# Long convolution and two dense layers on one core: four of sixteen weight chunks are decoded during the transform of u

## The chip, the core and the metric

The kernel runs on one core of a Trainium2 chip, as one launch. The metric is device time in microseconds, 1407.19 us as the median of three runs before the change. TensorE (PE), VectorE (DVE), ScalarE (ACT) and GpSimd (POOL) compute, each in its own fixed order of instructions; SyncE (SP) issues all DMAs, also in a fixed order, so that a DMA that has to wait holds up those behind it.

## The reference

```python
h_filt = (np.maximum(pos_emb @ w1, 0.0) @ w2) * np.exp(-0.01 * np.arange(S))[:, None]
u = x * v                                            # S = 12480 rows, D = 128 columns
y = np.fft.irfft(np.fft.rfft(u, n=2*S, axis=1) * np.fft.rfft(h_filt, n=2*S, axis=0)[None], n=2*S, axis=1)[:, :S]
x = (x * y).reshape(S, D)
h = np.maximum(x @ moe_w_in, 0.0); x = (h * h) @ moe_w_out            # 128 -> 2048 -> 128
h = x @ moe2_w_in                                                     # again 128 -> 2048 -> 128
return np.where(h > 0.0, h, np.exp(np.minimum(h, 0.0)) - 1.0) @ moe2_w_out
```

The four weight matrices arrive in float64, the rest in float32.

## The kernel before

The work has three phases.

**Phase 1** (`phase1`) is the first stage of the transforms. x and v come in 16 parts j of 8 columns each (`load_xv(j)`), into rotating buffers `xc` (x, ten of them) and `vc` (v, two of them; the first eight parts of v lie in tiles `m` that are written only later). `ufold(j)` multiplies and folds a part in three DVE instructions (lines 265, 266, 267; the last one is recorded at line 130). `s1(i)` is a group of 16 matmul records on PE (line 274) whose results ACT copies out of PSUM. There are 16 groups for the filter, then 32 for u, two for each part j. Ten parts are folded ahead of the groups for u, and after the groups of part j, part j + 10 is loaded and folded into the buffers that have come free. `prologue` issues eight small loads (`w2`, `g` and six of `tb`) after group 15, and the first matmuls of phase 2 after groups 24 and 29.

**Phase 2** (`phase2`) is a loop over 46 pairs p of frequencies. For each pair PE computes `u` (line 452, two PSUM buffers) and, two pairs later, the inverse stage `v` (line 475). In even pairs it also computes `rt` (line 319), in odd ones `h` (line 332) from `rr`, the copy that ACT makes of `rt`. ACT also copies `h` to `hh` and `v` to `z`; SP stores `z`. `prod(p)` is two products on DVE (lines 464, 465) and two sums on POOL (lines 467, 468), which give `pt` for `v`. DVE must have read `u` of pair p before PE can write `u` of pair p + 2, and `rr` must be copied before the next `h`.

Between these instructions a generator `weights()` puts the work on the 16 weight chunks (512 KB of float64 each, read as pairs of 32-bit words, `low` and `high`). It is stepped four times in each pair, once before `prod`, once after it, and twice more, and each step emits the next piece of one `decode` and of one `split`. `decode(c)` makes float32 out of the words: DVE masks the mantissa (373), ACT scales it (375), DVE shifts the exponent out (376), ACT limits it in two steps (379, 382), DVE adds the low word (381) and the sign (384), POOL multiplies mantissa and power (389). `split(c)` makes the high and low halves for the matmuls: ACT copies (recorded at 133, `m<-wf`), POOL subtracts (130, `m<-wf,m`). Decode c starts at step 11c or later, with at most four decoded chunks waiting for their split (`wf`, four buffers); splits start in pairs 8, 16 and 32, when the tiles `m` come free. Raw chunks have two buffers, and chunk c + 2 is loaded when DVE has last read chunk c. The order of instructions on each engine is the order in which the program writes them (`manual_schedule`).

The tiles of phase 2 (`raw`, `pt`, `m2`, `z` and others, pool `p2b`) lie in the memory of pool `xv`, which holds `xc` and `vc` in phase 1.

**Phase 3** (`phase3`) is the end of the inverse transform and the two layers, eight steps for each of 26 tiles of rows; it is not touched.

Of the kernel before, what the change touches and what calls it, by code (L numbers as in the profile page):

```python
# [10 lines left out]
F32 = mybir.dt.float32  # L11
F32R = mybir.dt.float32r
U32 = mybir.dt.uint32
AF = mybir.ActivationFunctionType
ALU = mybir.AluOpType
# [5 lines left out]
D = 128  # L21
# [9 lines left out]
R = 99  # L31
# [1 line left out]
SIZES = (4,) + 24 * (5,) + (3,)  # L33
KTAIL = K1 - 64
TBB = 6
WF = 4
PD = NP - 2
PZ = PD - 4
HD = (33, 35, 36, 37, 38, PZ + 2)
# [1 line left out]
WDEC = 11  # L41
OFF = 3
LAG1 = 2
NX = 10
NV = 2
NWARM = 6
NS1 = 55

# [71 lines left out]
class Build:  # L120
# [56 lines left out]
    def phase1(self):  # L177
        nc, a = self.nc, self.a
        with ExitStack() as ctx1:
# [5 lines left out]
            ns = [0]  # L185
# [15 lines left out]
            xvp = self.right.enter_context(self.tc.tile_pool(name="xv", bufs=1, side="right"))  # L201
# [10 lines left out]
            def load_xv(j):  # L212
                for i, (d, nm, n) in enumerate(((xs, "xc", NX), (vs, "vc", NV))):
                    if i and j < 8:
                        t = self.xu[j // 4][:R, 1024 * (j % 4):1024 * (j % 4) + 1024]
                    else:
                        t = xvp.tile([R, 1024], F32, tag=nm, name=nm, bufs=n)
                    d[j] = t.rearrange("p (d h n) -> p d h n", d=8, h=2)
                    for b, e in ((0, R - 1), (R - 1, R)):
                        nc.sync.dma_start(out=t[b:e], in_=a["xv"][j, i, b:e])  # L220
# [10 lines left out]
            for j in range(8):  # L231
                load_xv(j)
# [30 lines left out]
            def ufold(j):  # L263
                x, v = xs[j], vs.pop(j)
                nc.vector.tensor_tensor(out=v, in0=x, in1=v, op=ALU.mult)
                nc.vector.tensor_tensor(out=x[:, :, 0], in0=v[:, :, 0], in1=v[:, :, 1], op=ALU.add)
                self.sub(nc.vector, x[:, :, 1], v[:, :, 0], v[:, :, 1])

            def s1(i, fb, dst, w):
                ps = stile(2, 512)  # L270
                pv = ps[:, :, :4 * K1].rearrange("p b (c e) -> p b c e", e=2)
                for j in range(4):
                    for q, (b, e) in enumerate(((0, C1), (C1, N2))):
                        nc.tensor.matmul(pv[b:e, j // 2, :, j % 2], lhsT=fb[j][q], rhs=self.t1[:, :, q:q + 2],  # L274
                                         start=(j % 2 == 0), stop=(j % 2 == 1))
                b = 0
                for o, n in dst:
                    o = o.rearrange("p (c d) -> p c d", d=w)[:N2, :, 4 * i:4 * i + 4]
                    o, z = o.rearrange("p c (b e) -> p c b e", e=2), pv[:N2, :, b:b + n].rearrange("p b c e -> p c b e")
                    self.copy(o, z)  # L280
                    b += n

            for j in range(NX):
                ufold(j)
                if 8 <= j + 8 < NX:
                    load_xv(j + 8)
            for i in range(E // 4):
                s1(i, [(fold[:, 0, :, 4 * i + c], fold[:, 1, 1:, 4 * i + c]) for c in range(4)], [(self.xr, 2 * K1)], E)
            dst = [(t, n) for t, n in zip(self.xu + [self.xt], (32, 32, 64, 2 * KTAIL))]
            self.raw = {}  # L290
            for j in range(D // 8):
                x = xs.pop(j)
                for i in range(2 * j, 2 * j + 2):
                    s1(i, [(x[:, 4 * (i % 2) + c, 0], x[:, 4 * (i % 2) + c, 1, 1:]) for c in range(4)], dst, D)
                    self.prologue(i)
                if j + NX < D // 8:
                    load_xv(j + NX)
                    ufold(j + NX)

    def buf(self, tag, shape, bufs, dt=F32, pool=None):  # L300
        return (pool or self.p2).tile([128] + list(shape), dt, tag=tag, name=tag, bufs=bufs)
# [50 lines left out]
        if i == 29:  # L352
            self.hmm(0)

    def load_weights(self, c):
        l, k, q = c // 8, c // 4 % 2, c % 4
        raw = self.buf("raw", [4, D, 2], 2, U32, self.p2b)
        src = self.a[(("moe_w_in", "moe_w_out"), ("moe2_w_in", "moe2_w_out"))[l][k]].bitcast(U32)
        if k == 0:
            src = src[:, 1024 * q:1024 * q + 1024].rearrange("p (b d) -> p b d", d=2 * D)  # L360
        else:
            src = src[512 * q:512 * q + 512, :].rearrange("(b p) d -> p b d", p=128)
        self.nc.sync.dma_start(out=raw.rearrange("p a b c -> p a (b c)"), in_=src)
        self.raw[c] = raw

    def decode(self, c):
        nc = self.nc
        raw = self.raw.pop(c)
        low, high = raw[:, :, :, 0], raw[:, :, :, 1]
        e = self.buf("we", [4, D], 2, U32, self.p2b)  # L370
        f = self.buf("wf", [4, D], WF, pool=self.p2b)
        t, s, w, m = e.bitcast(F32), e, f, f.bitcast(U32)
        nc.vector.tensor_scalar(out=m, in0=high, scalar1=0xFFFFF, scalar2=None, op0=ALU.bitwise_and)
        yield
        nc.scalar.activation(out=f, in_=m, func=AF.Copy, scale=2.0 ** -20, bias=1.0)
        nc.vector.tensor_scalar(out=e, in0=high, scalar1=1, scalar2=21,
                                op0=ALU.logical_shift_left, op1=ALU.logical_shift_right)
        yield
        nc.scalar.activation(out=t, in_=e, func=AF.Relu, bias=self.ebias[:, 0:1], scale=-1.0)
        yield  # L380
        nc.vector.scalar_tensor_tensor(out=f, in0=low, scalar=2.0 ** -52, in1=f, op0=ALU.mult, op1=ALU.add)
        nc.scalar.activation(out=e, in_=t, func=AF.Relu, bias=self.ebias[:, 1:2], scale=-8388608.0)
        yield
        nc.vector.scalar_tensor_tensor(out=s, in0=high, scalar=0x80000000, in1=e,
                                       op0=ALU.bitwise_and, op1=ALU.bitwise_or)
        if c + 2 < 16:
            self.load_weights(c + 2)
        yield
        nc.gpsimd.tensor_tensor(out=w, in0=f, in1=s.bitcast(F32), op=ALU.mult)  # L389
        yield  # L390
        self.dec[c] = w

    def split(self, c):
        if c % 4 == 0:
# [11 lines left out]
        yield  # L406

    def weights(self):
        self.w, self.dec = {}, {}
        nd = ns = 0  # L410
        gd = gs = None
        i = 0
        while ns < 16 or gs is not None:
            if gd is None and nd < 16 and nd - ns < WF and i >= WDEC * nd:
                gd, nd = self.decode(nd), nd + 1
            if gs is None and ns < 16 and ns in self.dec and self.pair >= (8, 16, 32, 32)[ns // 4]:
                gs, ns = self.split(ns), ns + 1
            if gd is not None and next(gd, 0) == 0:
                gd = None
            if gs is not None and next(gs, 0) == 0:  # L420
                gs = None
            i += 1
            yield

    def phase2(self):
        nc, a, st = self.nc, self.a, self.st
        ctx0 = self.ctx
        with ExitStack() as self.ctx:
# [6 lines left out]
            x0 = self.x0pool.enter_context(self.tc.tile_pool(name="x0", bufs=1, side="right"))  # L435
            self.x0 = [x0.tile([128, n0 * (R - 1)], F32R, name=nm) for nm in ("xh0", "xl0")]
            self.p2b = p2b = self.right.enter_context(self.tc.tile_pool(name="p2b", bufs=1, side="right"))
            for c in range(2):
                self.load_weights(c)
            wgen = self.weights()  # L440

# [53 lines left out]
            n = sum(nrs)  # L495
# [358 lines left out]
```

## Time and profile before

| | us |
|---|---|
| median of three runs (lowest, highest) | 1407.19 (1406.85, 1408.92) |
| the profiled execution | 1408.68 |
| its span in the trace | 1406.9 |
| PE busy (share of the span) | 1372.3 (98%) |
| DVE, ACT, POOL busy | 1187.2, 1128.8, 615.3 |

The profiled execution is 1.5 us above the median of the runs, and its span is 1.8 us shorter than its time. Phase 1 ends near 91 us and phase 2 near 237 us. Records of PE are pipelined, so that their durations overlap; starts tell more than ends. A number in square brackets behind a row is the time its engine was idle ahead of it, with what ended that.

### The profile page before, as it was taken

The numbers are of one execution on the slowest core, as the hardware profiler recorded it, in microseconds if no ns is written. First come the engines' busy times: TensorE is split into PE (matmuls) and PEld (weight loads), VectorE is DVE, ScalarE is ACT, GpSimd is POOL, SyncE is SP. The second block draws the span as 40 slices with busy tenths as digits, with TensorE's granted clock in tenths as the row PEclk, the third lists the DMA queues.
The fourth block names the chain that finished last, engine by engine and source line by source line (L and its number), as shares of the span: only waits on it lengthen the run. The fifth ranks groups of instructions, "written<-read, shape, count | busy, mean of one in ns | idle before, by whom it ended". The sixth has DMA issues, their size and how long they took to land.

```text
span 1406.9 us, 19203 instructions
## 1 busy us (share of the span) xinstructions
PE 1372.3 (98%) x7240; PEld 1157.6 (82%) x7240; DVE 1187.2 (84%) x1259; ACT 1128.8 (80%) x1484; POOL 615.3 (44%) x341
## 2 busy tenths in 40 slices
PE   8999898999999999999999999999999999999997
PEld 7986665898888888888888888888888888888875
DVE  6648786789888898888988898898988898888887
ACT  5777665788888888888888888888888888888886
POOL 3028784644444444444444444444444444444431
PEclk9999999999999999999999999999999999999999
DMA  8746674201110111001110111001110111000000
GB/s 264 191 121 205 167 249 138 87 0 41 41 41 1 42 41 41 16 26 41 41 42 0 41 42 41 19 24 41 41 41 1 41 41 42 16 13 9 8 8 12
DMA packets 43165, 81.49 MB, mean 58 GB/s; under 512 B 3944, under 2 KB 32755, under 8 KB 43073
## 3 DMA queue, kind: packets, MB, share of 16 engines
q1 hardware_dynamic: 43073, 80.27, 18.9%
q8 instruction: 57, 0.93, 0.3%
q14 instruction: 35, 0.29, 0.1%
HBM read 61.90 MB, written 18.32 MB: 57 GB/s over the span
## 4 chain that ended last, share of the span: by engine, by line
PE 89%; DVE 3%; POOL 2%; ACT 2%; DMA 2%; issue 1%; SPq 0%; POOLq 0%; DVEq 0%; ACTq 0%
PE y L156 13%; PE h L155 12%; PE h L157 12%; PE y L157 12%; PE y L155 12%; PE h L156 12%; PE s L274 4%; PE h L580 4%; PE v L475 2%; PE u L452 2%; DMA m<-in_xv_dram 1%; PE h L332 1%; PE rt L319 1%; POOL pt L467 1%; POOL wf L389 1%
## 5 line engine op out<-in xcount | busy, mean ns | idle before, releaser
L130 POOL TENSOR_TENSOR lo<-g,hi 128x980 fp32r<-128x980 f32 (+4 forms) x206 | 483.0, 2345 | 657.3 <-DVE tn L770 615.7
L805 ACT ACTIVATE tn<-h 128x980 f32<-128x980 f32 (+4 forms) x208 | 202.9, 976 | 177.8 <-PE h L157 165.7
L770 DVE SCALAR_TENSOR_TENSOR tn<-ex,tn 128x980 f32<-128x980 f32 (+4 forms) x208 | 241.1, 1159 | 118.2 <-ACT ex L806 115.8
L156 PE MATMUL y<-lo,m 128*128 128x490 f32 (+4 forms) x832 | 318.0, 382 | 6.5 <-POOL lo L130 3.6
L155 PE MATMUL y<-hi,m 128*128 128x490 f32 (+4 forms) x832 | 319.7, 384 | 4.0 <-ACT hi L133 1.7
L155 PE MATMUL h<-xh,m 128*128 128x490 f32 (+4 forms) x832 | 317.3, 381 | 1.8 <-DVE g L780 1.0
L157 PE MATMUL y<-hi,m 128*128 128x490 f32 (+4 forms) x832 | 317.6, 382 | 0.0
L157 PE MATMUL h<-xh,m 128*128 128x490 f32 (+4 forms) x832 | 316.9, 381 | 0.0
L156 PE MATMUL h<-xl,m 128*128 128x490 f32 (+4 forms) x832 | 315.9, 380 | 0.2 <-DVE xl L130 0.2
L130 DVE TENSOR_TENSOR lo<-ex,hi 128x980 fp32r<-128x980 f32 (+5 forms) x208 | 257.3, 1237 | 1.1 <-ACT hi L133 1.0
L780 DVE SCALAR_TENSOR_TENSOR g<-h,r 128x980 f32<-128x980 f32 (+4 forms) x208 | 239.5, 1152 | 12.0 <-ACT r L776 11.8
L797 DVE SCALAR_TENSOR_TENSOR ex<-tn,h 128x980 f32<-128x980 f32 (+4 forms) x208 | 238.2, 1145 | 0.6
L133 ACT ACTIVATE hi<-ex 128x980 fp32r<-128x980 f32 (+4 forms) x208 | 211.9, 1019 | 2.0 <-DVE ex L797 1.9
L787 ACT ACTIVATE hi<-r 128x980 fp32r<-128x980 f32 (+4 forms) x208 | 211.8, 1019 | 0.9
L776 ACT ACTIVATE r<-h 128x980 f32<-128x980 f32 (+4 forms) x208 | 204.1, 981 | 8.0 <-PE h L157 7.9
L806 ACT ACTIVATE ex<-h 128x980 f32<-128x980 f32 (+4 forms) x208 | 201.1, 967 | 0.0
L156 PEld LDWEIGHTS y<-lo,m 128*128 128x128 f32 x832 | 156.8, 188 | 37.0 <-POOL lo L130 5.9
L155 PEld LDWEIGHTS y<-hi,m 128*128 128x128 f32 x832 | 157.1, 189 | 34.5 <-ACT ys L133 4.6
L155 PEld LDWEIGHTS h<-xh,m 128*128 128x128 f32 x832 | 156.8, 188 | 29.9 <-DVE g L780 2.0
L156 PEld LDWEIGHTS h<-xl,m 128*128 128x128 f32 x832 | 156.9, 189 | 27.7 <-DVE xl L130 0.4
L157 PEld LDWEIGHTS y<-hi,m 128*128 128x128 f32 x832 | 157.0, 189 | 26.7
L157 PEld LDWEIGHTS h<-xh,m 128*128 128x128 f32 x832 | 156.7, 188 | 26.8
(84 smaller groups left out, 1167.4 us busy)
## 6 DMA issues: line engine op xcount, KB each, us to landing
z<-Zd SPq DMA_DIRECT2D x24, 546.0 KB
Zd<-z SPq DMA_DIRECT2D x45, 256.0 KB
t<-in_t_dram SPq DMA_DIRECT2D x24, 351.9 KB
xc<-in_xv_dram SPq DMA_DIRECT2D x16, 392.0 KB
tb<-in_tf_dram SPq DMA_DIRECT2D x46, 127.0 KB
raw<-in_moe_w_in_dram SPq DMA_DIRECT2D x8, 512.0 KB
raw<-in_moe_w_out_dram SPq DMA_DIRECT2D x8, 512.0 KB
m<-in_xv_dram SPq DMA_DIRECT2D x8, 392.0 KB
```

Source lines behind the costliest of these rows:

```text
L130: return eng.tensor_tensor(out=out, in0=a, in1=b, op=ALU.subtract)
L133: self.nc.scalar.activation(out=out, in_=in_, func=AF.Copy)
L155: nc.tensor.matmul(out, lhsT=lhi, rhs=rhi, start=start, stop=False)
L156: nc.tensor.matmul(out, lhsT=lhi, rhs=rlo, start=False, stop=False)
L157: nc.tensor.matmul(out, lhsT=llo, rhs=rhi, start=False, stop=stop)
L770: after = nc.vector.scalar_tensor_tensor(out=pa["em"], in0=pa["ex"], scalar=1.0, in1=pa["tn"], op0=ALU.add, op1=ALU.mult)
L776: nc.scalar.activation(out=f["r"], in_=f["h"], func=AF.Relu)
L780: nc.vector.scalar_tensor_tensor(out=f["g"], in0=f["h"], scalar=0.0, in1=f["r"], op0=ALU.max, op1=ALU.mult)
L787: nc.scalar.activation(out=f["hi"], in_=f["r"], func=AF.Square)
L797: nc.vector.scalar_tensor_tensor(out=pa["g"], in0=pa["em"], scalar=0.0, in1=pa["h"], op0=ALU.min, op1=ALU.max)
L805: nc.scalar.activation(out=e["tn"], in_=e["h"], func=AF.Tanh, scale=0.5)
L806: nc.scalar.activation(out=e["ex"], in_=e["h"], func=AF.Exp)
```

## The change

Chunks 0 to 3 are loaded and decoded in phase 1. After the groups of part j = 6 to 9 chunks 0 to 3 are loaded, chunk 0 into a `vc` buffer, the others into `xc` buffers; after those of j = 7 to 10 they are decoded, with DVE in the place of ACT and POOL for the product as before. `xc` has nine buffers in place of ten, and `vc` has three in place of two, in pool `p2`, where it lives on through phase 2: the decoded chunks lie in it, two to a buffer, in place of `wf`.

Decode is changed for all chunks. The exponent and the power are written over the low word, so `we` is gone; the low word is therefore added before the shift, both in one step, and both steps on ACT follow in one step. The load of chunk c + 2 is issued after POOL's product is written in the program, since that product is now the last reader of the raw chunk. In phase 2 decode c starts at step 11(c - 4) or later, and the test for a free buffer goes by pairs of chunks.

```diff
-WF = 4
-NX = 10
-NV = 2
+NX = 9
+NV = 3
+NE = 4
@@ load_xv
-                        t = xvp.tile([R, 1024], F32, tag=nm, name=nm, bufs=n)
+                        t = (self.p2 if i else xvp).tile([128, 1024], F32, tag=nm, name=nm, bufs=n)[:R]
@@ loop over j, after load_xv(j + NX) and ufold(j + NX)
+                c = j + NX - D // 8 + 1
+                if 0 <= c < NE:
+                    pool, nm, n = (xvp, "xc", NX) if c else (self.p2, "vc", NV)
+                    self.load_weights(c, pool.tile([128, 1024], F32, tag=nm, name=nm, bufs=n).bitcast(U32))
+                if 1 <= c <= NE:
+                    for _ in self.decode(c - 1, nc.vector):
+                        pass
@@ decode
-        e = self.buf("we", [4, D], 2, U32, self.p2b)
-        f = self.buf("wf", [4, D], WF, pool=self.p2b)
-        t, s, w, m = e.bitcast(F32), e, f, f.bitcast(U32)
+        t = low.bitcast(F32)
+        if c % 2 == 0:
+            self.wf = self.buf("vc", [8, D], NV)
+        f = self.wf[:, 4 * (c % 2):4 * (c % 2) + 4]
+        m = f.bitcast(U32)
         nc.vector.tensor_scalar(out=m, in0=high, scalar1=0xFFFFF, scalar2=None, op0=ALU.bitwise_and)
         yield
-        nc.scalar.activation(out=f, in_=m, func=AF.Copy, scale=2.0 ** -20, bias=1.0)
-        nc.vector.tensor_scalar(out=e, in0=high, scalar1=1, scalar2=21,
+        if early:
+            early.tensor_scalar(out=f, in0=m, scalar1=2.0 ** -20, scalar2=1.0, op0=ALU.mult, op1=ALU.add)
+        else:
+            nc.scalar.activation(out=f, in_=m, func=AF.Copy, scale=2.0 ** -20, bias=1.0)
+        yield
+        nc.vector.scalar_tensor_tensor(out=f, in0=low, scalar=2.0 ** -52, in1=f, op0=ALU.mult, op1=ALU.add)
+        nc.vector.tensor_scalar(out=low, in0=high, scalar1=1, scalar2=21,
                                 op0=ALU.logical_shift_left, op1=ALU.logical_shift_right)
         yield
-        nc.scalar.activation(out=t, in_=e, func=AF.Relu, bias=self.ebias[:, 0:1], scale=-1.0)
+        if early:
+            early.tensor_scalar(out=t, in0=low, scalar1=896.0, scalar2=0.0, op0=ALU.subtract, op1=ALU.max)
+            early.tensor_scalar(out=low, in0=t, scalar1=255.0, scalar2=8388608.0, op0=ALU.min, op1=ALU.mult)
+        else:
+            nc.scalar.activation(out=t, in_=low, func=AF.Relu, bias=self.ebias[:, 0:1], scale=-1.0)
+            nc.scalar.activation(out=low, in_=t, func=AF.Relu, bias=self.ebias[:, 1:2], scale=-8388608.0)
         yield
-        nc.vector.scalar_tensor_tensor(out=f, in0=low, scalar=2.0 ** -52, in1=f, op0=ALU.mult, op1=ALU.add)
-        nc.scalar.activation(out=e, in_=t, func=AF.Relu, bias=self.ebias[:, 1:2], scale=-8388608.0)
+        nc.vector.scalar_tensor_tensor(out=low, in0=high, scalar=0x80000000, in1=low,
+                                       op0=ALU.bitwise_and, op1=ALU.bitwise_or)
         yield
-        nc.vector.scalar_tensor_tensor(out=s, in0=high, scalar=0x80000000, in1=e,
-                                       op0=ALU.bitwise_and, op1=ALU.bitwise_or)
-        if c + 2 < 16:
+        nc.gpsimd.tensor_tensor(out=f, in0=f, in1=t, op=ALU.mult)
+        yield
+        if NE <= c < 14:
             self.load_weights(c + 2)
-        yield
-        nc.gpsimd.tensor_tensor(out=w, in0=f, in1=s.bitcast(F32), op=ALU.mult)
-        yield
-        self.dec[c] = w
+        self.dec[c] = f
@@ weights
-        nd = ns = 0
+        nd, ns = NE, 0
-            if gd is None and nd < 16 and nd - ns < WF and i >= WDEC * nd:
+            if gd is None and nd < 16 and nd - nd % 2 - ns < 2 * NV - 1 and i >= WDEC * (nd - NE):
@@ phase2
-            for c in range(2):
+            for c in range(NE, NE + 2):
                 self.load_weights(c)
```

## Rows read from the trace of the kernel before

**Rows 1.** Waits, 90 to 250 us: who waited for whom, us in total, times, longest.
```profile
ACT m L133 <- POOL wf L389: 19.6, 8, 3.9
...
PE h L332 <- ACT rr L133: 6.1, 6, 2.2
...
PE u L452 <- DVE m L465: 2.4, 2, 2.3
DVE wf L373 <- POOL m L130: 2.3, 1, 2.3
```
**Rows 2.** Timeline of ACT: start, duration, line, operation, idle before.
```profile
158.59 0.63 ACT L133 ACTIVATE m<-wf 128x512 fp32r<-128x512 f32 x1 [2.79 <-POOL wf L389]
```
**Rows 3.** Timeline of PE in phase 2, where it stands still.
```profile
127.69 1.16 PE L332 MATMUL h<-w,rr 64*127 64x128 f32 x16 [1.02 <-ACT rr L133]
...
159.75 1.77 PE L332 MATMUL h<-w,rr 64*127 64x128 f32 x16 [2.19 <-ACT rr L133]
161.46 2.08 PE L475 MATMUL v<-pt,g 127*128 127x512 f32 x2
...
226.09 0.67 PE L452 MATMUL u<-xt,tb 127*127 127x256 f32 x2 [2.26 <-DVE m L465]
```
**Rows 4.** Timeline of PE in phase 2, where it runs through.
```profile
182.91 1.03 PE L452 MATMUL u<-m,tb 127*127 127x256 f32 x4
...
184.95 1.12 PE L475 MATMUL v<-pt,g 127*128 127x512 f32 x2
...
188.53 1.03 PE L452 MATMUL u<-xt,tb 127*127 127x256 f32 x4
189.48 1.16 PE L332 MATMUL h<-w,rr 64*127 64x128 f32 x16
```
**Rows 5.** Timeline of DVE, end of phase 1 and start of phase 2.
```profile
55.89 1.23 DVE L265 TENSOR_TENSOR vc<-xc,vc 99x1024 f32<-99x1024 f32 x1 [4.46 <-DMA xc<-in_xv_dram]
...
76.47 0.69 DVE L130 TENSOR_TENSOR xc<-vc 99x512 f32<-99x512 f32 x1
...
94.15 0.59 DVE L373 TENSOR_SCALAR wf<-raw 128x512 uint32<-128x512 uint32 x1 [0.71 <-DMA raw<-in_moe_w_in_dram]
...
98.18 0.68 DVE L464 TENSOR_TENSOR pt<-u,hh 127x512 f32<-127x512 f32 x1
```
**Rows 6.** Timeline of SP, the DMA issues at the end of phase 1.
```profile
69.72 1.20 SPq L346 DMA_DIRECT2D w<-in_w_dram  x2
...
71.61 4.17 SPq L305 DMA_DIRECT2D tb<-in_tf_dram  x6
89.91 0.80 SPq L363 DMA_DIRECT2D raw<-in_moe_w_in_dram  x2
```
**Rows 7.** Instructions that read the raw chunks, durations min/median/max in ns.
```profile
L373 DVE TENSOR_SCALAR wf<-raw x16: 501/640/1416, 94.2 to 216.8; 128x512 uint32<-128x512 uint32 x16
L376 DVE TENSOR_SCALAR we<-raw x16: 415/948/1494, 94.7 to 221.3; 128x512 uint32<-128x512 uint32 x16
L381 DVE SCALAR_TENSOR_TENSOR wf<-raw,wf x16: 662/876/1249, 96.2 to 222.1; 128x512 f32<-128x512 uint32 x16
L384 DVE SCALAR_TENSOR_TENSOR we<-raw,we x16: 692/848/1608, 97.6 to 224.1; 128x512 uint32<-128x512 uint32 x16
```
**Rows 8.** Timeline of POOL around 190 us.
```profile
189.20 0.73 POOL L467 TENSOR_TENSOR pt<-pt 127x256 f32<-127x256 f32 x1 [2.87 <-DVE pt L464]
...
191.92 1.27 POOL L130 TENSOR_TENSOR m<-wf,m 128x512 fp32r<-128x512 f32 x1
```
**Rows 9.** Timeline of DVE at the end of that subtraction.
```profile
193.22 0.93 DVE L373 TENSOR_SCALAR wf<-raw 128x512 uint32<-128x512 uint32 x1 [2.31 <-POOL m L130]
```
**Rows 10.** Groups of ACT instructions, 0 to 420 us: busy us, mean ns, idle before.
```profile
L133 ACT ACTIVATE rr<-rt 128x508 f32<-128x508 f32 (+1 forms) x22 | 12.8, 584 | 9.0 <-PE rt L319 8.9
...
L382 ACT ACTIVATE we<-we,ebias 128x512 uint32<-128x512 f32 x16 | 11.4, 716 | 0.2
L375 ACT ACTIVATE wf<-wf 128x512 f32<-128x512 uint32 x16 | 10.1, 629 | 4.0 <-DVE wf L373 3.9
```

More of the change, by code (lines that the diff above doesn't have):

```diff
@@ L289, in phase1 @@
             dst = [(t, n) for t, n in zip(self.xu + [self.xt], (32, 32, 64, 2 * KTAIL))]
-            self.raw = {}
+            self.raw, self.dec = {}, {}
             for j in range(D // 8):
@@ L353, in prologue, with load_weights @@
             self.hmm(0)
-    def load_weights(self, c):
+    def load_weights(self, c, raw=None):
         l, k, q = c // 8, c // 4 % 2, c % 4
-        raw = self.buf("raw", [4, D, 2], 2, U32, self.p2b)
+        if raw is None:
+            raw = self.buf("raw", [4, D, 2], 2, U32, self.p2b)
+        else:
+            raw = raw.rearrange("p (a b c) -> p a b c", a=4, c=2)
         src = self.a[(("moe_w_in", "moe_w_out"), ("moe2_w_in", "moe2_w_out"))[l][k]].bitcast(U32)
@@ L364, in load_weights, with decode @@
         self.raw[c] = raw
-    def decode(self, c):
+    def decode(self, c, early=None):
         nc = self.nc
@@ L377, in decode @@
+        nc.vector.tensor_scalar(out=low, in0=high, scalar1=1, scalar2=21,
                                 op0=ALU.logical_shift_left, op1=ALU.logical_shift_right)
         yield
-        nc.scalar.activation(out=t, in_=e, func=AF.Relu, bias=self.ebias[:, 0:1], scale=-1.0)
+        if early:
+            early.tensor_scalar(out=t, in0=low, scalar1=896.0, scalar2=0.0, op0=ALU.subtract, op1=ALU.max)
+            early.tensor_scalar(out=low, in0=t, scalar1=255.0, scalar2=8388608.0, op0=ALU.min, op1=ALU.mult)
+        else:
+            nc.scalar.activation(out=t, in_=low, func=AF.Relu, bias=self.ebias[:, 0:1], scale=-1.0)
+            nc.scalar.activation(out=low, in_=t, func=AF.Relu, bias=self.ebias[:, 1:2], scale=-8388608.0)
@@ L408, in weights @@
     def weights(self):
-        self.w, self.dec = {}, {}
-        nd = ns = 0
+        self.w = {}
+        nd, ns = NE, 0
         gd = gs = None
```

## The prediction

> **What bounds the kernel now.** I read the page first: PE is busy for nearly the whole span, so a change pays only where PE stands still. The slices and the stretches by stage then show where that is: phase 1 runs through, phase 3 is not touched, and the gaps lie in phase 2. The view of the waits in that phase names them [rows 1]. Its first line to look at is no wait of PE: ACT waited 19.6 us in eight pieces for line 389, POOL's last product of a decode. The copy of a split stands in ACT's fixed order right behind the decode of the same chunk; ACT stands still until POOL is done [rows 2], and the copy of `rt` behind it comes late. PE then waits for `rr`: 6.1 us in six pieces, and 2.4 us in two for the products on DVE that are late for the same reason [rows 1]. The timeline of PE shows three of them [rows 3]: 1.02 us at 127.69, 2.19 us at 159.75, 2.26 us at 226.09. After the second one the `h` took 1.77 us where the one at 127.69 took 1.16, and the `v` 2.08 us where a regular one takes 1.12 [rows 3, 4]; the engine had stood still ahead of it and ran at about half pace for these two, another 0.61 + 0.96 = 1.6 us. In all the stalls of phase 2 that hang on the decodes are worth 6.1 + 2.4 + 1.6 = 10.1 us. That is all that this change can take away; the work itself on DVE, ACT and POOL is not on the path.
>
> **What is removed: 10.1 us.** By the step rule, decode 15 ran at steps 165 to 171 before and its split came at 172; decodes 3, 6, 7, 13 and 14 ended just as tightly ahead of their splits. Stepping the new rule by hand, decodes 4 and 5 run from steps 0 and 11, decodes 6 to 9 from 34, 41, 48 and 55, 10 to 13 from 66, 77, 88 and 99, 14 and 15 from 130 and 137, while the splits start at 29, 33, 37, 41 (0 to 3), 61 to 73 (4 to 7) and 125 to 153 (8 to 15). No copy is closer than ten steps, or two and a half pairs, behind its product. I count the whole 10.1 us as gone.
>
> **What is added at the seam of the phases: 4.5 us.** With nine buffers, part 9 too is loaded only when PE has read a part of u, so seven parts instead of six are folded from 55.89 on. A part is 1.23 + 2 x 0.69 = 2.6 us of DVE; before, six of them took until 77.2, or 3.5 each, since a load of v had to wait for one of two buffers [rows 5]. Seven take between 7 x 2.6 and 7 x 3.55, so the last is folded between 74.1 and 80.7; with three buffers for v I take 75.5. PE reads the last part just ahead of 89.91 [rows 6], so that alone costs nothing. The load of chunk 0 waits in SP's order for the fold of part 13, two parts earlier, at 70.3. Behind it come the eight small loads, which kept SP for 6.1 us (69.72 to 75.78) [rows 6], so chunks 1 to 3 are issued at 76.4. Before, the first chunk was issued at 89.91 and DVE could start on it at 94.15, 4.2 us later [rows 5, 6]; so chunk 1 can be decoded from 80.6, with chunk 0 done by then. An early decode is seven instructions of DVE: the mask, four with one tensor operand (scale, shift, two limits) and two with two tensors. At the shortest of [rows 7] they take 0.50 + 4 x 0.42 + 0.66 + 0.69 = 3.5 us, at the medians 0.64 + 4 x 0.95 + 0.88 + 0.85 = 6.2. POOL has almost nothing else to do there, so I stay near the short end, with gaps between instructions that depend on each other: 4.1 us. Three of them end at 92.9, and POOL's product 1.3 us later [rows 8], at 94.2.
>
> The first load of phase 2 was issued at 89.91 [rows 6], the moment that PE was done with the last part of x, though the few KB of its two buffers can hardly lie under that one part; so I read that the tiles of `p2b` wait for the whole pool `xv`. That pool now holds chunks 1 to 3, and chunk 4 is issued at 94.2 and lands at 98.4. The mask of chunk 4 stands in DVE's order right behind the products of pair 0, so the products of pair 1, and `u` of pair 3 on PE, wait for that landing as they waited for 94.15 before: 4.3 us later. In the new decode the add stands ahead of the shift, and both steps on ACT ahead of the sign, so the products of pair 2 (98.18 before [rows 5]) come some 1 us later still; PE had almost as much to spare there. I take 4.5 us. Bounds: with a decode of 3.5 us 2.7, with 6.2 us 10.8; and if chunk 4 need not wait, only the products of pair 0 come late, by 92.9 against the end of phase 1, some 1 us.
>
> On the length of the early decode the shift of line 376 is telling: between 415 and 1494 ns [rows 7] for the same work. The Trainium skill says (SBUF — State Buffer, "SBUF: two separate sides") that a DVE instruction with two SBUF inputs or in a two-port mode and a GpSimd instruction exclude each other for a whole instruction. By it each early decode would lose at most the one product of POOL that runs beside it, 3.5 + 1.3 = 4.8 us, and the seam would cost 6.6 us in place of 4.5.
>
> **What is added inside phase 2: 7.5 us.** Decode 6 starts at step 34, right behind the products of pair 9, into the buffer of chunks 0 and 1, whose last reader is the subtraction of split 1, written one step later. So DVE waits for POOL there; decode 10 (step 66, pair 17, split 5) and decode 14 (step 130, pair 33, split 9) stand in the same place. I lay the order of the program on a regular odd pair, with its `u` at 182.91 as zero; the `h` two pairs on is at 189.48, or 6.57, and the next odd pair's `u` at 5.62 [rows 4]. The `u` takes 1.03 and the first product 0.68 [rows 5]: 1.7. POOL's two sums at 0.73 and gaps: 3.3; its subtraction 1.27 [rows 8]: 4.6. Only then the mask: 5.2. ACT's scale 0.63: 5.8. The add 0.7 and the shift 0.5 [rows 7]: 7.0. Two limits on ACT at 0.72: 8.5. Behind them in ACT's order stands the copy `rr`, 0.58 [rows 10]: 9.1. PE wants it at 6.57, so it waits 2.5 us, three times 7.5. The bounds: a wait of DVE for that subtraction, of 2.31 us, was there before [rows 9], with at most a small share of the 6.1 us behind it, so nothing; and if POOL is one subtraction late, 3.8 each, or 11.4. I take the sum of the order, because the mask that waited before had its shift directly behind it, not behind the add.
>
> After three idles of 2.5 us the half pace can come back: 1.6 us after an idle of 2.19, nothing after 2.26 [rows 3]. I count one, 1.6 us, between none and three (4.8).
>
> Chunks 6 to 9 are decoded seven steps apart, and a raw chunk is loaded only when POOL's product is done. From the sign of chunk 6 to the mask of chunk 8 there are ten steps, two and a half pairs of 2.81, or 7.0 us; the product ends 2 to 4 us behind the sign and the load takes 4.2, so DVE waits 0 to 1.2 us there and again for chunk 9. PE has two buffers of `u` between; I take 0.6 us for both. The other moves cost nothing by this reading: ACT and DVE do the same pieces, and the Z stores that queue on SP behind a later load have three buffers of `z`, 8 us, to hide in.
>
> **The sum.** -10.1 + 4.5 + 7.5 + 1.6 + 0.6 = +4.1 us. On the profiled execution's 1408.7 that is 1412.8; that execution is 1.5 above the median of the runs, so for the median I forecast 1411.3.
>
> **Rivals.** *Faster:* DVE's three waits for the subtraction leave PE alone, as the one before did [rows 9]: ACT reaches `rr` in time. Then 7.5 and 1.6 fall away, -5.0 us, 1402.2. It decides where such a wait costs PE less than about 1.7 us. For it: PE has two buffers of `u`, and there is such a row; against it: the order of ACT, in which `rr` stands behind both limits. *No change:* buffers of `xv` are freed one by one and chunk 4 lands at about 94; the seam costs 1, the sum is +0.6, 1407.8. Against it is the issue at 89.91. *Slower by more:* the early decode runs at the medians; the seam costs 10.8, the sum is +10.4, 1417.6. Against it: those medians were taken beside a busy POOL. *The early decodes bring nothing:* the splits do not wait in either case, so this is excluded by the step rule unless POOL falls behind by ten steps.
>
> **How the numbers follow.** Main case 0.42, the faster rival 0.25, no change 0.18, slower by more 0.09, and 0.06 for what I don't see. A measurement of this kernel can tell about 0.2%, 2.8 us, from no change. The main case has its own spread of about 3 us (the bounds of the seam and of the waits), so a third of it falls within 2.8 us; the no-change rival gives most of the rest there. Faster 0.25, same 0.29, slower 0.46. The range reaches from the faster rival to the slow decode: 1401.5 to 1417.5. The main case alone: 1408 to 1415.
>
> **What would show it.** Right: no wait of ACT for line 389 worth more than 1 us; the first mask of phase 2 near 98.4; three waits of DVE's mask for POOL's subtraction (near pairs 9, 17 and 33), each with a gap of PE ahead of `h`, released by `rr`. Wrong: chunk 4 issued near 90; the three gaps below 1 us each; or a run from pair 36 to the end that still has gaps.

## The result and the profile after

The changed kernel takes 1428.59 us (median of 6 runs, 1425.1 to 1431.74) against 1409.57 (6 runs, 1406.85 to 1413.61): 1.0129 times the time before, with an interval of 1.0106 to 1.0152. It is slower by 19 us where the prediction had 4.1. The ratios here and below leave out one execution, of 7750.64 us in g_two_old_later. The profiled execution took 1429.6, with a span of 1427.8. The rows of after below keep the program's names, but the lines have moved: the mask is L385 (before L373), the shift L393 (L376), the two ReLUs L400 and L401, the sign L403, POOL's product L406 (L389); `u` is L471, `h` L339, `v` L494, the products of a pair L483 and L484. In the experiments the lines move by a few more; the tiles and operations tell which is which.

First the view of the waits in phase 2, which answers to [rows 1] and [rows 9] (who waited for whom, us in total, times, longest):

```profile
ACT vc L390 <- DVE vc L385: 24.0, 8, 10.7
...
PE h L339 <- ACT rr L133: 17.1, 8, 4.8
...
DVE raw L403 <- ACT raw L401: 12.4, 12, 1.6
...
ACT raw L400 <- DVE raw L393: 10.1, 10, 1.8
...
DVE vc L385 <- POOL m L130: 9.3, 3, 4.4
PE u L471 <- DVE m L484: 6.8, 3, 6.2
```

ACT's wait for POOL's product, 19.6 us before, is not there any more. In its place PE waits for `rr` 17.1 us (6.1 before) and DVE's mask waits three times for POOL's subtraction (9.3 in three, 2.3 in one before). Two more rows have grown: the first ReLU waits for the shift on DVE, 10.1 us in ten pieces, and the sign on DVE for the second ReLU, 12.4 in twelve. In the same view of before they were:

```profile
DVE we L384 <- ACT we L382: 6.0, 8, 1.2
...
ACT we L379 <- DVE we L376: 2.0, 4, 0.8
```

Where PE stands still, from its timeline (start, duration, operation, idle before and what ended it). [Rows 3] answer to these:

```profile
100.55 2.04 PE L471 MATMUL u<-m,tb 127*127 127x256 f32 x4 [6.24 <-DVE m L484]
102.38 1.79 PE L326 MATMUL rt<-tb,xr 127*128 127x127 f32 x8
...
108.63 1.16 PE L339 MATMUL h<-w,rr 64*127 64x128 f32 x16 [2.52 <-ACT rr L133]
...
133.72 1.26 PE L339 MATMUL h<-w,rr 64*127 64x128 f32 x16 [2.54 <-ACT rr L133]
134.91 2.07 PE L494 MATMUL v<-pt,g 127*128 127x512 f32 x2
...
148.62 1.16 PE L339 MATMUL h<-w,rr 64*127 64x128 f32 x16 [1.96 <-ACT rr L133]
...
166.43 2.08 PE L339 MATMUL h<-w,rr 64*127 64x128 f32 x16 [4.75 <-ACT rr L133]
168.44 2.08 PE L494 MATMUL v<-pt,g 127*128 127x512 f32 x2
...
217.85 1.16 PE L339 MATMUL h<-w,rr 64*127 64x128 f32 x16 [2.55 <-ACT rr L133]
```

To see what each gap is worth, I took the start of the `u` of every pair in both timelines, counted from the `u` of pair 0 (90.93 before, 90.33 after), and subtracted. The end of phase 2 is taken at the first matmul that reads the last `pt`. The lateness grows at six places and shrinks where a stall of before has gone:

| place | forecast, us | lateness gained after |
|---|---|---|
| seam: pairs 2 to 4 | +4.5 | +10.7 |
| decodes 6, 10, 14 with the half pace (pairs 12 to 13, 20 to 21, 36) | +7.5 + 1.6 | +4.3 + 7.5 + 2.4 = +14.2 |
| decodes 8, 9 and 12 (pairs 16 to 18, 26) | +0.6 | +4.9 |
| everything else, nearly all stalls of before that are gone | -10.1 | -11.7 |
| end of phase 2 | +4.1 | +18.0 |

So phase 2 accounts for the result, and the sum missed by 13.9 us: 6.2 at the seam, 5.1 at the three waits, 4.3 at other decodes, less 1.6 of gain.

Now the seam. DVE in after (answers to [rows 5]):

```profile
84.53 0.43 DVE L385 TENSOR_SCALAR vc<-xc 128x512 uint32<-128x512 uint32 x1 [1.97 <-DMA xc<-in_moe_w_in_dram]
85.00 0.43 DVE L388 TENSOR_SCALAR vc<-vc 128x512 f32<-128x512 uint32 x1
...
88.73 1.40 DVE L388 TENSOR_SCALAR vc<-vc 128x512 f32<-128x512 uint32 x1
...
97.03 0.69 DVE L403 SCALAR_TENSOR_TENSOR xc<-xc 128x512 uint32<-128x512 uint32 x1
99.11 0.69 DVE L483 TENSOR_TENSOR pt<-u,hh 127x512 f32<-127x512 f32 x1 [1.39 <-POOL vc L406]
...
103.24 0.43 DVE L385 TENSOR_SCALAR vc<-raw 128x512 uint32<-128x512 uint32 x1 [2.83 <-DMA raw<-in_moe_w_out_dram]
```

POOL's last early product, in the timeline of POOL in after (answers to [rows 8]):

```profile
97.80 1.28 POOL L406 TENSOR_TENSOR vc<-vc,xc 128x512 f32<-128x512 f32 x1 [3.27 <-DVE xc L403]
```

SP's issues of the weight chunks in after (answer to [rows 6]):

```profile
72.42 0.36 SPq L373 DMA_DIRECT2D vc<-in_moe_w_in_dram  x1
...
78.51 1.32 SPq L373 DMA_DIRECT2D xc<-in_moe_w_in_dram  x3
99.11 0.93 SPq L373 DMA_DIRECT2D raw<-in_moe_w_out_dram  x2
```

Chunk 4 is issued at 99.11, right at the end of POOL's last early product (97.80 + 1.28 = 99.08), and so does the first product of pair 0 start, which before ran as soon as PE had given it its `u`, at about 92. Nothing else ends there: the whole pool is waited for, as the prediction read it.

### The profile page after: what moved, and what is told of

The parts are those of the page before. It is cut to its first block, busy times and chain, and to the rows that moved or that the text cites. A ratio compares the mean times of both kernels' runs of the same rounds, so it can differ in the third digit from the quotient of the medians.

```text
span 1427.8 us, 19233 instructions
## 1 busy us (share of the span) xinstructions
PE 1378.2 (97%) x7240; PEld 1161.3 (81%) x7240; DVE 1185.3 (83%) x1271; ACT 1124.9 (79%) x1472; POOL 609.3 (43%) x341
## 4 chain that ended last, share of the span: by engine, by line
PE 84%; DVE 5%; DMA 3%; ACT 3%; issue 2%; POOL 2%; SPq 1%; POOLq 0%; DVEq 0%; ACTq 0%
PE h L155 12%; PE y L156 12%; PE h L157 12%; PE y L157 12%; PE y L155 12%; PE h L156 12%; PE h L599 4%; PE s L274 2%; DMA vc<-in_xv_dram 1%; PE v L494 1%; PE u L471 1%; PE h L339 1%; DMA xr<-in_post_dram 1%; POOL m L130 1%; ACT raw L400 1%
```

## The experiments

Lateness at the seam is measured in all runs alike, counted from the `u` of pair 0: how much later than before the first mask of phase 2 starts (before 3.2 us behind that `u`), and how much later the `u` of pair 4 (before 9.6). Each ratio is to the kernel before, on the same chip. "Old order" means the decode of before. The theory drawn from the two traces, ahead of these runs: the loss is a sum of three, 10.7 us at the seam, some 14 in the three waits for the subtraction and some 5 from the new order inside the decode, through ACT's fixed order, less 11 us gained. The rival: the order is the main loss, and the three waits only make it visible.

**a_order: the new order alone.** Before, with all its buffers and loads, but with the decode of the change.

```diff
-        e = self.buf("we", [4, D], 2, U32, self.p2b)
+        t = low.bitcast(F32)
...
-        nc.vector.tensor_scalar(out=e, in0=high, scalar1=1, scalar2=21,
...
         nc.vector.scalar_tensor_tensor(out=f, in0=low, scalar=2.0 ** -52, in1=f, op0=ALU.mult, op1=ALU.add)
-        nc.scalar.activation(out=e, in_=t, func=AF.Relu, bias=self.ebias[:, 1:2], scale=-8388608.0)
+        nc.vector.tensor_scalar(out=low, in0=high, scalar1=1, scalar2=21,
...
+        nc.scalar.activation(out=t, in_=low, func=AF.Relu, bias=self.ebias[:, 0:1], scale=-1.0)
+        nc.scalar.activation(out=low, in_=t, func=AF.Relu, bias=self.ebias[:, 1:2], scale=-8388608.0)
...
-        nc.gpsimd.tensor_tensor(out=w, in0=f, in1=s.bitcast(F32), op=ALU.mult)
+        nc.gpsimd.tensor_tensor(out=f, in0=f, in1=t, op=ALU.mult)
...
+        if c + 2 < 16:
+            self.load_weights(c + 2)
```

> The kernel before, with the new order inside each decode alone (the add ahead of the shift, exponents over the low words, both ReLUs in one step, the next load behind POOL's product); nothing is decoded early and the buffers are those of before. Theory (the loss is a sum of three: 10.7 us at the seam of the phases, some 14 us in three waits of DVE for POOL's subtraction, some 5 us because rr stands behind both ReLUs, which stand behind add and shift; 11 us are gained): about 5 us over the kernel before, with extra gaps of PE of 0.5 to 2 us ahead of h, released by rr, spread over the decodes. Rival (the order of the decode is the main loss, and the three waits only make it visible): 12 us or more over the kernel before. Rival (the order costs nothing): within 2 us.

Measured: 1418.97 us, ratio 1.0064 [1.0046, 1.0082], some 9 us slower, between the theory's 5 and the 12 of its first rival. Its waits in phase 2:

```profile
DVE raw L384 <- ACT raw L382: 16.8, 16, 1.7
...
ACT raw L381 <- DVE raw L378: 16.3, 12, 1.9
...
PE h L332 <- ACT rr L133: 13.0, 10, 2.3
```

PE's wait for `rr` doubles against [rows 1], in ten pieces, without one early chunk. The order costs this by itself; ACT's timeline of this run shows how:

```profile
129.71 0.63 ACT L375 ACTIVATE wf<-wf 128x512 f32<-128x512 uint32 x1
130.23 0.59 ACT L133 ACTIVATE rr<-rt 128x508 f32<-128x508 f32 x1
132.70 0.78 ACT L381 ACTIVATE raw<-raw,ebias 128x512 f32<-128x512 uint32 x1 [1.88 <-DVE raw L378]
```

The shift now stands behind the add, and the add behind ACT's scale. So the first ReLU waits 1.88 us for DVE, and all that is behind it in ACT's order waits too, the copies of `rr` and `hh` of later pairs among it.

**l_relus: a_order with the two ReLUs in two steps again**, so that other copies of ACT can come between them; the decode is one step longer by it.

```diff
         nc.scalar.activation(out=t, in_=low, func=AF.Relu, bias=self.ebias[:, 0:1], scale=-1.0)
+        yield
         nc.scalar.activation(out=low, in_=t, func=AF.Relu, bias=self.ebias[:, 1:2], scale=-8388608.0)
```

> The kernel before with the new order inside the decode (as in the first run of this list), but with the two ReLUs on ACT in two steps instead of one. Theory (rr is late because both ReLUs stand ahead of it in one step): the loss of 9 us is about halved, 3 to 6 us over the kernel before. Rival (rr is late because the shift, and with it the first ReLU, waits for the add and that for ACT's scale): the loss stays, 7 us or more over the kernel before.

Measured: 1414.87, ratio 1.0038 [1.0023, 1.0052], +5.4 us where a_order had +9. In its waits PE's for `rr` goes from 13.0 us to 9.9:

```profile
ACT raw L381 <- DVE raw L378: 20.5, 13, 2.3
...
PE h L332 <- ACT rr L133: 9.9, 11, 1.7
```

The two ReLUs in one step are some four of the nine microseconds. The shift behind the add stayed in this run, with 20.5 us of waits of the first ReLU for it; I take it for the rest, by argument.

**d_oldorder: the change, with the old order in phase 2**, and one buffer for the exponents. The early decodes are as in after.

```diff
+        if not early:
+            e = self.buf("we", [4, D], 1, U32, self.p2b)
...
+            nc.scalar.activation(out=f, in_=m, func=AF.Copy, scale=2.0 ** -20, bias=1.0)
+            nc.vector.tensor_scalar(out=e, in0=high, scalar1=1, scalar2=21,
...
+            nc.scalar.activation(out=t, in_=e, func=AF.Relu, bias=self.ebias[:, 0:1], scale=-1.0)
+            yield
+            nc.vector.scalar_tensor_tensor(out=f, in0=low, scalar=2.0 ** -52, in1=f, op0=ALU.mult, op1=ALU.add)
+            nc.scalar.activation(out=e, in_=t, func=AF.Relu, bias=self.ebias[:, 1:2], scale=-8388608.0)
...
+            if NE <= c < 14:
+                self.load_weights(c + 2)
+            yield
+            nc.gpsimd.tensor_tensor(out=f, in0=f, in1=t, op=ALU.mult)
...
+            return
```

> The changed kernel, but in phase 2 the decode has the order of before (exponents in a buffer of their own, of which there is one; shift beside the mask's scale, the ReLUs in two steps, the load behind the sign); the four early decodes, the buffers and the start of each decode stay. Theory of three parts: the 5 us of the order go, and the three waits cost about half, since the shift no longer stands behind the add: 8 to 12 us less than the changed kernel; the seam keeps its 10. Rival (the waits for the subtraction cost their whole price in any order): 5 us less. Rival (the order is the main loss): 16 us or more less.

Measured: 1419.31, ratio 1.0068 [1.0043, 1.0092], against 1.0129 of after: 9 us given back, as the theory had it. In its waits, DVE still stands three times for POOL's subtraction, but it costs PE less:

```profile
DVE vc L387 <- POOL m L130: 8.5, 3, 3.6
PE h L339 <- ACT rr L133: 8.4, 7, 2.8
```

8.5 us of DVE's waits (9.3 in after), but 8.4 of PE's (17.1). At decode 6 both can be read side by side. In after the mask starts at 129.33 and `rr` at 133.09, 3.76 us later; in this run it is 127.96 and 130.81, 2.85 later. PE's gap ahead of that `h` is 2.54 in after and 1.62 here: the same 0.9 us less. DVE at decode 6 in d_oldorder, with the shift right behind the mask:

```profile
127.96 0.43 DVE L387 TENSOR_SCALAR vc<-raw 128x512 uint32<-128x512 uint32 x1 [2.44 <-POOL m L130]
128.31 0.42 DVE L390 TENSOR_SCALAR we<-raw 128x512 uint32<-128x512 uint32 x1
```

And ACT there, `rr` behind the decode's pieces:

```profile
130.81 0.57 ACT L133 ACTIVATE rr<-rt 128x508 f32<-128x508 f32 x1
```

The lateness gained at decodes 6, 10 and 14 falls from 14.2 us to 1.7 + 2.8 + 1.5 = 6.0, and at the seam from 10.7 to 8.5. At the close decodes it hardly falls, from 4.9 to 4.0 (pairs 15 to 17): there the shift of decode 8 waited 1.84 us, at 142.28, for POOL's product of decode 7, which still read the one buffer for the exponents.

**b_later: the change, where a decode starts at least four steps behind the subtraction that frees its buffer** (`se[c]` is the step of that subtraction).

```diff
-            if gd is None and nd < 16 and nd - nd % 2 - ns < 2 * NV - 1 and i >= WDEC * (nd - NE):
+            if gd is None and nd < 16 and i >= max(WDEC * (nd - NE), self.se.get(nd - nd % 2 - 5, 999) + KW if nd > 5 else 0):
```

> The changed kernel, but a decode that takes a buffer over starts four steps (one pair) behind the subtraction that reads it last, instead of one step ahead of it. Theory of three parts: the three waits of DVE (2.45, 4.44 and 2.45 us) fall below 1 us each and the gaps of PE behind them go, 12 to 14 us less than the changed kernel. Rival (those gaps come from the order inside the decode, which is the same here): DVE waits less, but PE still stands ahead of h, at most 4 us less.

Measured: 1424.65, ratio 1.0099 [1.0084, 1.0114], only some 4 us below after, as the rival had it. DVE's waits for POOL's subtraction fall from 9.3 us in three pieces to one of 1.6, and PE's for `rr` from 17.1 to 7.8, by the waits of b_later:

```profile
PE h L340 <- ACT rr L134: 7.8, 8, 1.7
...
DVE vc L386 <- POOL m L131: 1.6, 1, 1.6
```

Yet phase 2 ends 15.3 us late: 9.5 from the seam, and the rest at other decodes, +9.4 at pairs 15 to 23 and +4.7 at 40 and 41, less what is gained. Taking most of the waits away did not take their cost away. These decodes still have the new order, and decodes 6 to 9 still stand close together; which of the two brought the cost back is not told apart here.

**c_two and c_three: two or three early chunks.**

```diff
-NE = 4
+NE = 2
```

In c_three the number is 3.

> The changed kernel with two early chunks in place of four. The last early decode then ends before PE is done with phase 1, so the seam should be clean, and by the step rule decodes 6, 10 and 14 start ten steps or more behind the subtraction of their buffer, or one step behind it (14). Theory of three parts: the seam's 10.7 us and most of the 14 us of waits go, 20 to 25 us less than the changed kernel, so some 3 to 6 us below the kernel before, with only gaps ahead of h left that come from the order. Rival (the order is the main loss): 11 us less than the changed kernel, the seam alone.

> The changed kernel with three early chunks. What is looked at is the seam alone. Theory (the seam's length is set by the end of the last early decode, whose product frees the pool for chunk 3's load): with one early decode less, 4.4 to 4.7 us, the first load of phase 2 is issued near 94.4, and the start of u in pair 4 comes 4 to 5 us earlier than in the changed kernel (near 106). Rival (buffers of the pool are freed one by one, and the load waits for something else): the load stays near 99, or falls to 90 at once.

Measured: c_two 1414.95, ratio 1.0033 [1.0022, 1.0044], +4.8 us; c_three one run, 1417.68. With three, the first product of pair 0 and the first load of phase 2, issued at 93.41, move to the end of the third POOL product (expected near 94.4). DVE in c_three:

```profile
93.41 0.69 DVE L483 TENSOR_TENSOR pt<-u,hh 127x512 f32<-127x512 f32 x1 [1.40 <-POOL vc L406]
...
97.60 0.43 DVE L385 TENSOR_SCALAR vc<-raw 128x512 uint32<-128x512 uint32 x1 [2.90 <-DMA raw<-in_moe_w_in_dram]
```

The seam costs 6.9 us with three, 1.3 with two. But c_two is still slower than before; its expectation, which put it below, was wrong. The lateness of 6.2 us at pairs 36 and 37, at decode 14, where DVE waits 5.0 us for the subtraction, and small gaps elsewhere take the gain away.

**k_small_first: the change, with the eight small loads issued in the first group for u**, so that chunks 1 to 3 need not stand behind them.

```diff
-        if i == 15:
+        if i == 0:
```

> The changed kernel, with the eight small loads (w2, g, six of tb) issued at the first group for u, where SP stands idle, in place of behind the load of chunk 0. Theory (the early decodes are late because chunk 1's load stands behind those issues; DVE stood idle for 2.0 us between the decodes of chunks 0 and 1): chunk 1 is issued 5 to 6 us earlier, DVE goes through without that idle time, and the seam is 2 to 3 us shorter; the rest stays. Rival (the loads of u's parts are delayed by the small ones, and the folds with them): no gain at the seam.

Measured: 1425.74, ratio 1.0113 [1.0097, 1.0130], a seam of 11.5 us. Chunks 1 to 3 are issued at 72.25 in place of 78.51, and DVE goes from decode 0 to decode 1 without idling, but decode 0 itself starts at 79.05 (78.81 in after), and decode 1 now meets a POOL product. DVE in k_small_first:

```profile
82.73 0.41 DVE L385 TENSOR_SCALAR vc<-xc 128x512 uint32<-128x512 uint32 x1
83.17 1.41 DVE L388 TENSOR_SCALAR vc<-vc 128x512 f32<-128x512 uint32 x1
...
98.28 0.69 DVE L483 TENSOR_TENSOR pt<-u,hh 127x512 f32<-127x512 f32 x1 [1.39 <-POOL vc L406]
```

No gain at the seam, as the rival had it. The first product comes 0.8 us earlier than in after, of 1.8 at the start of decode 1. With the queue out of the way, DVE's own chain of folds and four decodes sets the seam almost as late, and PE ran longer at half pace behind it (`rt` 1.91 and `v` 1.79 us, 1.79 and 1.02 in after).

**e_two_old: two early chunks and the old order in phase 2** (the edits of c_two and d_oldorder together), **g_two_old_later: that with the rule of b_later as well.**

> Two early chunks in place of four, and in phase 2 the decode in the order of before (with its own buffer for the exponents). Theory, as mended by the first runs (the seam costs about 9 us, the order inside the decode about 9, the start one step ahead of a subtraction the rest; about 11 us of waits are gained): only the start of decode 14 one step ahead of its subtraction is left, 2 to 5 us, so 5 to 9 us below the kernel before. Rival (the gain of 11 us was never there; the stalls of before were only moved): within 3 us of the kernel before.

> The run above, with each decode that takes a buffer over started four steps behind the last subtraction from it. Theory: the last gap, at decode 14, goes too: 8 to 11 us below the kernel before and 2 to 4 below the run above. Rival (in the old order a wait for the subtraction is covered by PE's two buffers): no difference from the run above.

Measured: e_two_old 1404.24, ratio 0.9958 [0.9946, 0.9971]; g_two_old_later 1403.92, ratio 0.9956 [0.9941, 0.9970]. Both beat both kernels. In e_two_old the seam is gone (the `u` of pair 4 comes 9.6 us behind that of pair 0, as before), and PE waits for `rr` once, by the waits of e_two_old:

```profile
DVE vc L387 <- POOL m L130: 5.0, 1, 5.0
...
PE h L339 <- ACT rr L133: 2.4, 1, 2.4
```

That is decode 14; the lateness gained there is 3.6 us, and phase 2 ends 6.2 us earlier than before. In g_two_old_later DVE's wait at decode 14 is 2.0 us and PE's two for `rr` are 2.3 together; phase 2, counted from its start, ends 7.9 us earlier, but the runs do not tell it from e_two_old. It was expected to gain 2 to 4 more and did not show it.

**h_four_spread: four early chunks, the old order, the rule of b_later, and decodes 6 to 13 eleven steps apart.**

```diff
-            if gd is None and nd < 16 and nd - nd % 2 - ns < 2 * NV - 1 and i >= WDEC * (nd - NE):
+            if gd is None and nd < 16 and i >= max(WDEC * (nd - NE) if nd < 6 else 38 + WDEC * (nd - 6) if nd < 14 else 0, self.se.get(nd - nd % 2 - 5, 999) + KW if nd > 5 else 0):
```

> Four early chunks as in the change, but in phase 2 the decode in the order of before, started at least four steps behind the subtraction that frees its buffer, and eleven steps apart where the change had seven (decodes 6 to 13 start from step 38 on). All that is left of the change's costs should be the seam. Theory (seam, order, early starts and close starts add up, and the stalls of before are gone): u of pair 4 comes 8 to 10 us late against the kernel before, nothing else of more than 1.5 us is added in phase 2, and the 11 us gained make it 0 to 4 us below the kernel before, 4 to 8 above the best one with two early chunks. Rival (four early decodes bring more relief than two): as fast as the one with two early chunks.

Measured: 1407.06, ratio 0.9979 [0.9970, 0.9988], 3 us below before. PE's wait for `rr` is 0.3 us in all, and its longest for a product on DVE is the one at the seam:

```profile
PE u L497 <- DVE m L510: 4.1, 1, 4.1
...
PE h L340 <- ACT rr L134: 0.3, 1, 0.3
```

What is left of the loss is the seam, 7.1 us; phase 2 ends 4.7 us early all the same, so 11.8 us of stalls were gained elsewhere. Against d_oldorder (1.0068) the later and wider decodes are worth 12 us. Against two early chunks, four are still the worse by about 3.

**f_nine: before, with decodes nine steps apart in place of eleven.** It has the distance between product and split in part, without the early chunks.

```diff
-WDEC = 11
+WDEC = 9
```

> The kernel before with decodes nine steps apart in place of eleven: no early decode and no other change, but chunks 3, 6, 7, 13 and 14 are decoded four steps or more ahead of their split instead of two. Theory (the stalls of before come from splits that stand right behind their decode, not from the amount of work): most of ACT's 19.6 us of waits for line 389 go, and 3 to 7 us below the kernel before. Rival (the work in phase 2 is too much for ACT, DVE and POOL, and only less of it helps): no gain, within 2 us, or slower, since the same work is packed closer.

Measured: 1413.34, ratio 1.0027 [1.0017, 1.0036], slower, as the rival had it. ACT's waits for POOL's product all but vanish, and others take their place, by the waits of f_nine:

```profile
PE h L332 <- ACT rr L133: 7.4, 7, 2.2
...
DVE wf L373 <- POOL m L130: 5.3, 2, 3.1
...
PE v L475 <- POOL pt L468: 4.3, 5, 1.8
...
ACT m L133 <- POOL wf L389: 3.7, 1, 3.7
```

19.6 us of ACT's waits fall to 3.7 and PE's wait for `rr` grows from 6.1 to 7.4. Distance alone is no gain where the same sixteen decodes are packed closer; that the chunks decoded early are what makes room in phase 2 is my reading of it; e_two_old and h_four_spread fit it, but no run tests it alone.

## Why the prediction was wrong

**The step that failed** is one sentence: "The other moves cost nothing by this reading: ACT and DVE do the same pieces". They do the same pieces in a longer chain. The order was used where a decode waited for the subtraction, and for "some 1 us" at the seam, but every decode of phase 2 has it, and ACT has its copies behind it. Three pairs of kernels that differ in this order, and in what goes with it (the place of one load, the buffer of the exponents), say what it costs: a_order against before +9 us; after against d_oldorder 1.0129 against 1.0068, 9; c_two against e_two_old 1.0033 against 0.9958, 10 to 11. Part of these nine was in the sum, in the 7.5 us of the three waits. By places, d_oldorder is without 2.2 us of the miss at the seam, all 5.1 at the three waits and 0.9 at the close decodes: at most 8.2 of the 15.6 us by which the three places together missed. The rest is the size of the seam and the close decodes, below.

**The gain of 10.1 us was about right.** No wait of ACT for line 406 is in phase 2, and 11.7 us came back in after; h_four_spread gains 11.8.

**The seam was read rightly and sized wrongly: 10.7 for 4.5.** Chunk 4 was issued when POOL was done with chunk 3, so the rival that frees `xv` buffer by buffer is out, and c_three moved it with that product. The landing came at 103.24, not 98.4, 4.1 us behind its issue as foreseen (4.2). The lateness of 4.8 us arose earlier: chunk 1 was decodable at 84.53, not 80.6, because the folds ahead of chunk 0's load ran later (72.42 for 70.3, so 78.51 for 76.4 for the next three), and these took 6.0 us to come, not 4.2. The early decodes took 3.75 us (chunk 1, without a product of POOL beside it), 4.68 and 4.76 in place of 4.1; the prediction had 4.8 for such a one as its other figure, and did not take it into the sum. The scale took 0.43 us alone at 85.00 and 1.40 at 88.73, where POOL's product ran from 88.46 to 89.85, and k_small_first shows the same. The Trainium skill (SBUF — State Buffer, "SBUF: two separate sides") says that whichever of a GpSimd instruction and a DVE instruction of certain kinds starts first holds the shared ports to its end; the trace agrees, as the scale ends 0.28 us behind the product.

The pool is not most of this lateness. DVE was at work on the early decodes until 97.72; counted from the `u` of pair 0 it was free for the first product 7.39 us in, where before that product ran 1.22 us in (92.15 less 90.93): 6.2 us later. The wait for POOL's product added 1.39 us and the landing of chunk 4 another 2.1 (2.83 of idle for 0.71 [rows 5]): together the 9.7 us by which the first mask is late. So the bound of "some 1 us", for a chunk 4 that need not wait, was too low as well. On PE the 10.7 us are 6.3 of the first stop, 1.7 at half pace behind it (`u` 2.04 and `rt` 1.79 us, where they took 1.03 and 1.05 before) and 2.7 of a second stop; the sum had half pace only behind the three waits.

The second stop is where "PE had almost as much to spare there" failed, for the same reason as the first step. In us, counted as said:

| run | order in phase 2 | first mask late | `u` of pair 4 late |
|---|---|---|---|
| after | new | 9.7 | 10.7 |
| k_small_first | new | 8.9 | 11.5 |
| b_later | new | 8.5 | 9.5 |
| c_three | new | 4.0 | 6.9 |
| c_two | new | -0.2 | 1.3 |
| a_order | new | 0.2 | 1.2 |
| d_oldorder | old | 9.0 | 8.5 |
| h_four_spread | old | 7.7 | 7.1 |
| e_two_old | old | -0.2 | 0.0 |

With the old order PE comes as late as the mask, or half a microsecond less; with the new one 1 to 3 us later. Where it is nearly 3, in c_three and k_small_first, half pace is part of it (in c_three `h` 2.08, `v` 2.07 and `u` 1.91 us behind the second stop). In after ACT stood 10.7 us at its scale for that mask, with both ReLUs ahead of `rr`, and PE waited a second time, 2.52 us at 108.63.

**The three waits were found in their places, and two of the three gaps had the forecast length**: 2.54 and 2.55 for 2.5. The gap at decode 10 was 4.75 us, beyond the bound of 3.8: POOL worked without a break from 155.30, where it began the product of decode 9, to the end of the subtraction at 162.01, and DVE waited 4.44 us for it. After the gaps of 2.54 and 4.75 the half pace came back, twice and not once: `v` took 2.07 and 2.08 us where it takes 1.12, the `u` behind it 1.66 and 1.91 where it takes 1.03 [rows 4], and `h` 2.08 us behind the longer one. That is 1.7 + 2.8 = 4.5 us for the forecast 1.6, and with the gaps themselves, 9.8 for 7.5, the three cost 14.2 us for 9.1. With the old order they cost 6.0; without most of DVE's waits, in b_later, only 4 us came back in all.

**The close decodes cost 4.9 us, not 0.6, and not by the way foreseen.** DVE waits once for a raw load, 2.8 us at the seam. At decode 8 of after it is again ACT's order. ACT in after:

```profile
146.08 0.75 ACT L400 ACTIVATE raw<-raw,ebias 128x512 f32<-128x512 uint32 x1 [1.72 <-DVE raw L393]
146.86 0.74 ACT L401 ACTIVATE raw<-raw,ebias 128x512 uint32<-128x512 f32 x1
...
147.99 0.58 ACT L133 ACTIVATE rr<-rt 128x508 f32<-128x508 f32 x1
```

The ReLU waits 1.72 us for the shift, `rr` comes at 147.99, and PE's gap at 148.62 is 1.96. But the old order alone does not take this away (4.0 us in d_oldorder, with its one exponent buffer); eleven steps apart, in h_four_spread, nothing is lost at these decodes.

**The rivals.** The faster one is out: each of the three waits cost PE more than the 1.7 us from which it decides. No change is out by the issue at 99.11. The slower one had the right side, and with 10.8 us even the seam's number, but by luck: its early decodes of 6.2 us were not seen.

**What stays open.** The split of the seam between DVE's chain and the release of the pool is read from one trace; no run with another place for the chunks tests it. Nor do the runs part the cost of close decodes from that of their order: d_oldorder changed the order but has one buffer for the exponents, b_later changed only the starts. Whether the rule of g_two_old_later gains anything over e_two_old lies below what the runs tell. The spans of the two profiled executions differ by 20.9 us and phase 2 by 18.0 less 0.6 for its earlier start; the other 3.5 lie behind phase 2, whose code the change leaves alone, and the runs of after scatter by 6.6.

## What to carry to other kernels

When an edit saves a buffer by writing in place, draw the chain of dependences across the engines that it makes and look at what stands behind each link in an engine's fixed order: here the same eight instructions cost 9 us more when the shift had to follow the add and both ReLUs came in one step, and no count of busy time shows it. Work moved into an idle stretch pays only as far as it is over when that stretch ends; with two chunks it was (ratio 0.9958, with the old order), with four DVE still had decodes to do, and the next load waited for a pool that they kept occupied. Where one edit bundles an early start with a new order, try each alone before the sum.

## What the runs showed of the hardware

The same DVE scale took 0.43 us or 1.40, by whether POOL's product of 1.39 us ran beside it, so an early decode was 1 us longer beside it.

PE came out of a wait at half pace, and not after every one. Windows of after (stretch, length, busy time and instructions of PE, PEld, DVE, ACT, POOL, granted clock, DMA share, GB/s):

```profile
166.50:170.40 3.90, 3.90 (x19) 2.64 (x20) 2.24 (x4) 2.43 (x4) 3.27 (x4) 0.50 0.33 93
...
176.00:186.00 10.00, 10.00 (x56) 7.01 (x56) 7.22 (x10) 6.73 (x10) 6.23 (x7) 1.00 0.39 120
```

Behind the 4.75 us of idle the granted clock is 0.50, the 1.2 GHz level, for the `h` and the `v`; ten microseconds on it is 1.00, 2.4 GHz. Behind the 6.24 us of the seam it is 0.51 from 100.50 to 104.00. The wait of 2.54 us at 133.72 was followed by a `v` of 2.07 us, the one of 2.55 at 217.85 by an `h` of 1.16 and a `v` of 1.12; in [rows 3] it is the same with 2.19 and 2.26.
